# One fused attention, expert and feed-forward kernel: weight tiles converted earlier, token tiles scaled earlier, sums stored in quarters

## The chip, the cores and the metric

The kernel runs on one core of a Trainium2 chip. The metric is the device time of one execution in microseconds. A core has a matrix engine (TensorE, PE in the rows), VectorE (DVE), ScalarE (ACT), GpSimd (POOL) and SyncE (SP), each with an instruction queue of its own that is worked off in order. SyncE computes nothing here: it issues most of the transfers between DRAM and the on-chip memory, and GpSimd issues the rest.

## The reference

Three layers follow one another on 2304 tokens (4 batches of 576), 512 wide. All arrays are 32-bit floats.

```
proj = x @ w_phi; proj -= max|proj|; phi = concat(exp(proj), exp(-proj))      # for q and for k
x    = (phi(q) @ (phi(k).T @ v)) / (phi(q) @ sum(phi(k)) + 1e-6)              # attention, 32 heads
e    = argmax(normalised x . normalised expert_emb)                           # one of 8 experts a token
x    = gate * (relu(x @ w1[e]) @ w2[e])                                       # w1 512x1024, w2 1024x512
h    = x @ w_in;  g = h * sigmoid(h);  out = g @ w_out                        # w_in 512x2048, w_out 2048x512
```

`w_in` and `w_out` arrive as 64-bit floats (the host hands their bytes over as 64-bit whole numbers), so the kernel turns them into 32-bit floats itself.

## The kernel before

A product of 32-bit floats is made of three matmuls in the fast format: each operand is split into a rounded high part (a copy on ScalarE) and the rest (a subtraction on VectorE), and high x high, low x high and high x low are added up (lines 781 to 783). So every block of weights costs a ScalarE copy and a VectorE subtraction before TensorE may use it.

**Slots.** After the attention the tokens are sorted by expert into 22 slots of 128. Slot s fetches its tokens (`gather`), turns them (`xturn`, tile `pxt`), multiplies by w1 (`mm1`, four steps k), applies relu, turns again (`hturn`) and multiplies by w2 (`mm2`, four steps i). The program interleaves neighbours: in round s stand `mm1(s, 0..3)`, then `mm2(s-1, 0..3)`, and between their steps the splits of the next weights (`split(s+1, 1, k)`, `split(s, 2, i)`). The expert weights come in through SyncE (`load1`, `load2`, tiles `raw`); a load is skipped where the expert stays the same.

**Conversion.** `narrow` turns one 128-column tile of `w_in` (or 128 rows of `w_out`) from 64 to 32 bits in four steps, one on ScalarE (line 194) and three on VectorE (lines 199 to 206); `cload` fetches a raw tile, `cwork` does the next step, `cstore` writes the result to DRAM. Tiles 0 to 9 of `w_in` are converted during the attention, 10 to 13 in rounds 5 to 16 (three rounds each), 14 and 15 in units 1 and 2 of the last layer (`sload`). `add_weights` lets GpSimd add stored tiles up in DRAM (three transfers per pair of tiles, each waiting for the one before).

**Units.** The last layer takes the tokens in four blocks of 576 (k) and `w_in` in eight pairs of tiles (q): 32 units u = 8k + q. In a unit seven products stand in for eight (Strassen's scheme in Winograd's form). The order in `unit` is 1, 5, 4 of the unit before, 6, 3 of the unit before, 2, 7. Products 1, 6, 7 and 4 run on in one accumulator `puA`, and after each `keep` copies it out on ScalarE (line 1062) before TensorE may add to it again; products 5, 3 and 2 are added by `join` on VectorE (line 1067). The results stand in two tiles of half a unit, `ha` and `hb`, four buffers in all, and `hstore` writes each to DRAM when both of its halves are in (`hd`, line 1073, SyncE).

`wfetch`, `whigh`, `wlow` bring in and split a pair of `w_in` tiles for a unit. `xfetch`, `xscale`, `xprep` bring in a token tile of a block (tile `yt`), scale it by its gate on VectorE (only the first six tiles of all, line 979) and turn it on TensorE (`pt`, line 988), after which ScalarE copies it out of the one bank that `pt` and `pxt` share (line 994). Block 0 goes through this in rounds 18 to 20, where all of it stands behind a step i of `mm2`. What else stands between the products of a unit is set by hand: `at(u, n, task)` puts a task behind product n of unit u. The 16 tiles of `w_out` are converted in units 8 to 26 that way (`oload` behind product 7 of the unit before, the four steps of `cwork` behind products 1, 5, 3 and 2).

Before unit 17 a branch (`tc.If`, line 1562) decides whether three spare slots are needed (`rest`); with these inputs it is not taken. After the units, 18 token tiles go through the gate and the product with `w_out` (`gate`, `down`, `finish`).

Of the kernel before, what the change touches and what calls it, by code (L numbers as in the profile page):

```python
# [19 lines left out]
P = 128  # L20
# [46 lines left out]
def moe_kernel(ctx, tc, qk, v, w_phi, emb, tau, w1, w2, win, wout, out):  # L67
# [172 lines left out]
    def phase_all(ctx):  # L240
# [686 lines left out]
        def cwork(i):  # L927
            if len(J[i]) == 2:
                J[i].append(narrow(J[i][0], J[i][1], nc.scalar, i))
            next(J[i][2], None)  # L930

        def cstore(i):
            keep_weights(i, J.pop(i)[1])

# [120 lines left out]
        def htile(u, name):  # L1055
            if (u, name) not in HT:
                HT[u, name] = pools["ur"].tile([P, 2, TN], F32, tag="h", name="h" + name, bufs=4)
            return HT[u, name]

        def keep(u, n):  # L1060
            b, name, half = {1: ("A", "a", 0), 6: ("A", "a", 1), 7: ("A", "b", 1), 4: ("A", "b", 0)}[n]
            nc.scalar.copy(out=htile(u, name)[:, half], in_=BK[u, b])

        def join(u, n):
            b, name, half = {5: ("C", "b", 1), 3: ("C", "a", 1), 2: ("B", "a", 0)}[n]
            o = htile(u, name)[:, half]
            nc.vector.tensor_tensor(out=o, in0=BK[u, b], in1=o, op=ALU.add)

        def hstore(u):
            k, q = divmod(u, NJP)  # L1070
            for odd, name in ((1, "b"), (0, "a")):
                dma = nc.gpsimd if u == NUNIT - 1 else nc.sync
                dma.dma_start(out=hd[k][2 * q + odd], in_=HT.pop((u, name)).rearrange("p a t -> p (a t)"))

        def unit(u, todo, skip=()):
            v = u - 1
            for n, w in ((1, u), (5, u), (4, v), (6, u), (3, v), (2, u), (7, u)):
                live = 0 <= w < NUNIT
                if live and (n, w) not in skip:
                    prod(w, n)  # L1080
                if live and n in (1, 6, 7, 4):
                    keep(w, n)
                if n == 5 and v >= 0:
                    join(v, 5)
                if live and n in (3, 2):
                    join(w, n)
                if live and n == 3:
                    hstore(v)
                for f, *a in todo.pop((u, n), ()):
                    f(*a)  # L1090
# [5 lines left out]

        def sload(i):
            if "s" not in J:
                J["s"] = pools["ur"].tile([P, 7 * 512], F32, tag="wb", name="wbs", bufs=4)
            o = (i % 2) * 1024  # L1100
            J[i] = [J["s"][:, o:o + 1024].bitcast(I32).rearrange("p (f t) -> p f t", t=2),
                    J["s"][:, 2048 + o // 2:2560 + o // 2].bitcast(I32)]
            fetch_raw(i, J[i][0])
# [305 lines left out]
        for s in range(1, NSF + 1):  # L1409
# [7 lines left out]
            if s < NSF:  # L1417
# [3 lines left out]
                if q < NJP - 1:  # L1421
                    add_weights(q, n)
                i, n = divmod(s - 5, 3)
                i += CA
                if s == 4:
                    cload(CA)
                for k in range(4):
                    mm1(s, k)
                    if (s, k) == RANK:
                        ranks(B - 1, rbank)  # L1430
                    route(1, s, k)
                    if s + 1 < NSF and k < 3:
                        split(s + 1, 1, k)
                    if 5 <= s < 17 and k == 1 and n == 0:
                        cwork(i)
                    if s == NSF - 1:
                        for f, *a in TAIL[k]:
                            f(*a)
# [13 lines left out]
            for i in range(4):  # L1452
# [11 lines left out]
                if i == 1 and 5 <= s < 17:  # L1464
                    cwork(CA + (s - 5) // 3)
                if i in (1, 2) and 18 <= s < 21:
                    n = 2 * (s - 18) + i - 1
                    if n < 5:
                        xscale(0, n)
# [9 lines left out]
            if 5 <= s < 17 and (s - 5) % 3 == 2:  # L1479
                i = CA + (s - 5) // 3  # L1480
                cstore(i)
                if s < 16:
                    cload(i + 1)
# [15 lines left out]
        htile(0, "a")  # L1499
        wfetch(2)  # L1500
        wfetch(3)
        sload(14)
        sload(15)
# [3 lines left out]
        def plan():  # L1507
            for q in range(2, NJP):
                at(q - 2, 6, whigh, q)
                at(q - 1, 5, wlow, q)  # L1510
                if q + 2 < NJP - 1:
                    at(q - 1, 4, wfetch, q + 2)
            at(5, 1, wfetch, NJP - 1)
# [45 lines left out]
        for u in range(NUNIT):  # L1559
            if u == 17:  # L1560
# [57 lines left out]
```

## Time and profile before

| | |
|---|---|
| median of 3 runs | 1013.27 us (1011.70 to 1014.08) |
| profiled execution, its own time | 1012.02 us |
| its span, first to last instruction | 1010.3 us |
| TensorE busy | 927.1 us, 92% |
| VectorE, ScalarE, GpSimd busy | 613.0, 588.0 and 250.3 us |
| mean granted TensorE clock | 0.97 of full speed |

The span has four stretches: the attention (to about 240 us), the slots (to about 555), the units (to about 800) and the products with `w_out` (to the end). Times in rows count from the start of the span. A wait row says which engine and line waited for which, then the sum, the number of times and the longest, in us.

### The profile page before, as it was taken

To read this page: it belongs to the slowest core of one execution; us is meant where nothing else is said; L and a number is where in the kernel's file an instruction comes from. 1 tells how busy PE (TensorE), PEld (TensorE's weight loads), DVE (VectorE), ACT (ScalarE), POOL (GpSimd) and SP (SyncE) were. 2 spreads that over 40 slices of the span, in tenths; PEclk is the share of its full clock that TensorE was granted. 3 is DMA by queue.
4 is the path that set the end of the run, shared out by engine and by line. 5 is a ranking of instruction groups with operands and counts; after the bars stand their busy time and mean duration, and the time that the engine had idled before them with its cause. 6 is when DMAs were issued, how large, how long until landed. Compare 5 with 4: busy or idle time off the path is not lost. (4 is left out here: it accounts for less than half of the span.)

```text
span 1010.3 us, 15487 instructions
## 1 busy us (share of the span) xinstructions
PE 927.1 (92%) x5567; PEld 801.6 (79%) x5567; DVE 613.0 (61%) x948; ACT 588.0 (58%) x963; POOL 250.3 (25%) x219
## 2 busy tenths in 40 slices
PE   8999999999999999999669596997988899999996
PEld 6999999977777777777557586886987888888885
DVE  6888897877999897797557353552554321112120
ACT  6778878648786897697556343442444443343441
POOL 6887878322015121221000030101000000010100
PEclk9999999999999999999789797998998999999999
DMA  6444534477579559739751784654666654333320
GB/s 177 137 135 143 151 106 132 142 283 219 157 232 259 144 177 336 246 72 290 260 177 42 234 230 143 212 197 152 228 227 208 218 156 138 104 105 115 104 73 21
DMA packets 117697, 173.90 MB, mean 172 GB/s; under 512 B 29736, under 2 KB 71848, under 8 KB 117616
## 3 DMA queue, kind: packets, MB, share of 16 engines
q1 hardware_dynamic: 105584, 151.00, 46.0%
q0 software_dynamic: 11952, 21.83, 9.5%
q8 instruction: 45, 0.74, 0.3%
q14 instruction: 36, 0.29, 0.1%
q10 hardware_dynamic: 80, 0.03, 0.0%
HBM read 172.05 MB, written 54.26 MB: 224 GB/s over the span
## 5 line engine op out<-in xcount | busy, mean ns | idle before, releaser
L831 DVE TENSOR_TENSOR wl<-raw,wh 128x1024 fp32r<-128x1024 f32 (+1 forms) x166 | 188.6, 1174 | 58.8 <-ACT wh L830 53.4
L830 ACT CAST wh<-raw 128x1024 fp32r<-128x1024 f32 (+1 forms) x166 | 160.5, 1032 | 31.4 <-DMA raw<-w 16.2
L1156 DVE TENSOR_TENSOR hlt<-gt,hlt 128x1024 fp32r<-128x1024 f32 x34 | 41.7, 1226 | 139.3 <-ACT hlt L1155 139.3
L782 PE MATMUL po<-wob,hlt 128*128 128x512 f32 x272 | 108.5, 399 | 0.0
L781 PE MATMUL po<-wob,hlt 128*128 128x512 f32 x272 | 107.2, 394 | 0.0
L783 PE MATMUL po<-wob,hlt 128*128 128x512 f32 x272 | 106.6, 392 | 0.0
L417 POOL TENSOR_TENSOR kl<-ke,kh 128x640 fp32r<-128x640 f32 x52 | 84.0, 1637 | 30.8 <-issue 23.2
L467 PE MATMUL pnx<-kv,qp 128*128 128x73 f32 x640 | 76.7, 275 | 0.0
L816 POOL DMA_INDIRECT xg<-xd,gidx x22 | 32.1, 1458 | 175.6 <-PE pxt L851 126.8
L1176 ACT COPY os<-po 128x512 f32<-128x512 f32 x17 | 10.0, 586 | 112.0 <-PE po L783 112.0
L467 PEld LDWEIGHTS pnx<-kv,qp 128*128 128x128 f32 x640 | 74.1, 192 | 0.1
L781 PE MATMUL ph<-wh,xh 128*128 128x512 f32 x166 | 67.1, 404 | 0.0
L783 PE MATMUL ph<-wh,xl 128*128 128x512 f32 x166 | 65.4, 394 | 0.6 <-DVE xl L838 0.4
L971 POOL DMA_INDIRECT yt<-yd,yidx x13 | 15.3, 1181 | 199.7 <-PE pt L988 156.9
L782 PE MATMUL ph<-wl,xh 128*128 128x512 f32 x166 | 64.8, 390 | 0.0
L378 DVE TENSOR_REDUCE m<-pqk 128x10 f32<-128x1280 f32 x32 | 47.5, 1485 | 24.3 <-PE pqk L372 22.9
L1177 POOL DMA_INDIRECT out<-os,oidx x18 | 17.5, 974 | 179.1 <-ACT os L1176 174.2
L781 PEld LDWEIGHTS po<-wob,hlt 128*128 128x128 f32 x272 | 51.1, 188 | 13.3
L783 PEld LDWEIGHTS po<-wob,hlt 128*128 128x128 f32 x272 | 51.1, 188 | 12.3
L782 PEld LDWEIGHTS po<-wob,hlt 128*128 128x128 f32 x272 | 51.1, 188 | 11.6
L372 PE MATMUL pqk<-wbd,zh 128*128 128x256 f32 (+1 forms) x320 | 59.5, 285 | 0.8 <-DVE d L379 0.6
L402 ACT ACTIVATE ke<-d 128x640 f32<-128x640 f32 x52 | 38.3, 737 | 36.8 <-DVE d L379 36.8
(407 smaller groups left out, 2503.6 us busy)
## 6 DMA issues: line engine op xcount, KB each, us to landing
raw<-w SPq DMA_DIRECT2D x44, 1536.0 KB
raw<-w SPq DMA_DIRECT2D x44, 512.0 KB
gt<-hd SPq DMA_DIRECT2D x11, 1024.0 KB
z<-qk SPq DMA_DIRECT2D x32, 288.0 KB
hd<-hb SPq DMA_DIRECT2D x31, 288.0 KB
hd<-ha SPq DMA_DIRECT2D x31, 288.0 KB
wo<-wout SPq DMA_DIRECT2D x16, 512.0 KB
yd<-ys SPq DMA_DIRECT2D x23, 256.0 KB
```

The costliest lines, as they stand in the source:

```text
L372: nc.tensor.matmul(out=pqk[0:r, c * 256:(c + 1) * 256], lhsT=z[:, c * P:c * P + r], rhs=wbd[:, j].rearrange("p h f -> p (h f)"), start=(i ...
L378: nc.vector.tensor_reduce(out=m, in_=pv, axis=AX.X, op=ALU.max, apply_absolute_value=True)
L402: nc.scalar.activation(out=ke, in_=kd, func=AF.Exp, scale=1.0 - 2.0 * s)
L417: nc.gpsimd.tensor_tensor(out=kl[:, :, s, :], in0=st.pop(("ke", g, s)), in1=kh[:, :, s, :].bitcast(F32), op=ALU.subtract)
L467: nc.tensor.matmul(out=pn[:, c, 0:73], lhsT=qp[:, s, c * P:(c + 1) * P], rhs=kv[:, s, 0:73], start=(s == 0), stop=(s == 1))
L781: nc.tensor.matmul(out=o, lhsT=ah, rhs=bh, start=first, stop=False, skip_group_check=more)
L782: nc.tensor.matmul(out=o, lhsT=ah, rhs=bl, start=False, stop=False, skip_group_check=more)
L783: nc.tensor.matmul(out=o, lhsT=al, rhs=bh, start=False, stop=last, skip_group_check=more)
L816: nc.gpsimd.indirect_dma_start(out=xg, out_offset=None, in_=xd[0:n, :], in_offset=bass.IndirectOffsetOnAxis(ap=gidx[:, p:p + 1], axis=0))
L830: nc.scalar.copy(out=hi[:, 0:n], in_=sl[:, 0:n])
L831: nc.vector.tensor_tensor(out=lo[:, 0:n], in0=sl[:, 0:n], in1=hi[:, 0:n].bitcast(F32), op=ALU.subtract)
L1156: nc.vector.tensor_tensor(out=lo, in0=g, in1=hi.bitcast(F32), op=ALU.subtract)
```

## The change

It has six edits.

- **Conversion in the slots.** `convert` does one step each half round from round 2 on, five half rounds per tile (four steps, then the store and the next load). So all six tiles 10 to 15 are done by round 16, where four were before. `sload` and the conversion in units 1 and 2 go; the last pair's `add_weights` stand in round 21.
- **Scaling apart from turning.** `xscale` of block 0 stands behind `mm1` steps 2 and 3, `xprep` behind `mm2` steps 2 and 3 (both stood behind steps 1 and 2 of `mm2`).
- **Quarters.** `ha` and `hb` become single sums `ht` of 128x288, eleven buffers, each stored as soon as its last copy or addition is done: four transfers of 144 KB a unit in place of two of 288 KB.
- **`w_out`.** The step of line 194 is done on VectorE (line 196), the four steps stand in pairs behind products 3 and 2, and the load three or four products earlier, behind product 4. The list of units leaves out two units of 19 where it left out three, so it now has 17 entries: the last one, unit 26, converts tile 0 of `w_out` once more and writes the same values.
- **Token tiles** 0 and 1 of blocks 1 to 3 are fetched behind product 1 in place of 7 of unit 8(k-1)+1, and the last pair of `w_in` behind product 4 of unit 4 in place of product 1 of unit 5.
- **The branch** stands before unit 7.

```diff
         def cwork(i):
             if len(J[i]) == 2:
-                J[i].append(narrow(J[i][0], J[i][1], nc.scalar, i))
+                J[i].append(narrow(J[i][0], J[i][1], nc.scalar if i < NJ else nc.vector, i))
             next(J[i][2], None)
...
+        def convert(n):
+            i, n = divmod(n - 4, 5)
+            if not 0 <= i < NJ - CA:
+                return
+            if n < 4:
+                cwork(CA + i)
+            else:
+                cstore(CA + i)
+                if CA + i + 1 < NJ:
+                    cload(CA + i + 1)
...
-        def htile(u, name):
-            if (u, name) not in HT:
-                HT[u, name] = pools["ur"].tile([P, 2, TN], F32, tag="h", name="h" + name, bufs=4)
-            return HT[u, name]
+        def htile(u, at):
+            if (u, at) not in HT:
+                HT[u, at] = pools["ur"].tile([P, TN], F32, tag="h", name="ht", bufs=11)
+            return HT[u, at]
...
+            nc.scalar.copy(out=htile(u, at), in_=BK[u, "A"])
+            if n == 4:
+                hstore(u, at)
...
             nc.vector.tensor_tensor(out=o, in0=BK[u, b], in1=o, op=ALU.add)
-        def hstore(u):
+            hstore(u, at)
...
+            dma = nc.gpsimd if u == NUNIT - 1 else nc.sync
+            dma.dma_start(out=hd[k][2 * q + at[0]][:, at[1] * TN:(at[1] + 1) * TN], in_=HT.pop((u, at)))
...
-                if q < NJP - 1:
-                    add_weights(q, n)
...
+                add_weights(q, n)
+                if s == NSF - 1:
+                    for q, n in ((NJP - 1, 0), (NJP - 1, 1), (NJP - 1, 2)):
+                        add_weights(q, n)
...
-                    if 5 <= s < 17 and k == 1 and n == 0:
-                        cwork(i)
+                    if k == 1:
+                        convert(2 * s)
+                    if k > 1 and 18 <= s < 21 and 2 * (s - 18) + k - 2 < 5:
+                        xscale(0, 2 * (s - 18) + k - 2)
...
-                if i in (1, 2) and 18 <= s < 21:
-                    n = 2 * (s - 18) + i - 1
+                if i == 1 and s < NSF:
+                    convert(2 * s + 1)
+                if i > 1 and 18 <= s < 21:
+                    n = 2 * (s - 18) + i - 2
                     if n < 5:
-                        xscale(0, n)
                         xprep(0, n)
...
-            for i in (14, 15):
-                for n in (1, 5, 3, 2):
-                    at(i - 13, n, cwork, i)
-                at(i - 13, 7, cstore, i)
-            for n, (u, m) in enumerate(((2, 7), (3, 6), (4, 1))):
-                at(u, m, add_weights, NJP - 1, n)
...
-                at(u + 1, 7, xfetch, k, 0)
-                at(u + 1, 7, xfetch, k, 1)
+                at(u + 1, 1, xfetch, k, 0)
+                at(u + 1, 1, xfetch, k, 1)
...
-            units = [u for u in range(8, 27) if u not in (15, 17, 23)]
+            units = [u for u in range(8, 27) if u not in (15, 23)]
             for j, u in enumerate(units):
-                at(u - 1, 7, oload, j)
+                at(u - 1, 4, oload, j)
             for j, u in enumerate(units):
-                for n in (1, 5, 3, 2):
+                for n in (3, 3, 2, 2):
                     at(u, n, cwork, NJ + j)
...
-            if u == 17:
+            if u == NJP - 1:
```

Three places show how instructions move. The first is VectorE in round 18, from the token tile of slot 19 (`xl`) to the end of `hturn(18)` (`hl`); `wl1` and `wl2` are split weights, `yt` the scaled token tiles. Before:

```order
L838 TENSOR_TENSOR xl_6019<-pxt_6013,xh_6018 128x512
L831 TENSOR_TENSOR wl1_6024<-raw1_1_2791,wh1_6023 128x1024
L831 TENSOR_TENSOR wl2_6045<-raw2_0_158,wh2_6044 128x1024
L831 TENSOR_TENSOR wl2_6075<-raw2_0_158,wh2_6074 128x1024
L979 TENSOR_SCALAR yt_5884<-yt_5884,gate_s_142 128x512
L831 TENSOR_TENSOR wl2_6096<-raw2_0_158,wh2_6095 128x1024
L979 TENSOR_SCALAR yt_5886<-yt_5886,gate_s_142 128x512
L831 TENSOR_TENSOR wl2_6113<-raw2_0_158,wh2_6112 128x512
```

The same place in the changed kernel:

```order
L990 TENSOR_SCALAR yt_5898<-yt_5898,gate_s_142 128x512
L990 TENSOR_SCALAR yt_5900<-yt_5900,gate_s_142 128x512
L838 TENSOR_TENSOR xl_6035<-pxt_6029,xh_6034 128x512
L831 TENSOR_TENSOR wl1_6040<-raw1_0_2790,wh1_6039 128x1024
L831 TENSOR_TENSOR wl2_6061<-raw2_0_158,wh2_6060 128x1024
L831 TENSOR_TENSOR wl2_6091<-raw2_0_158,wh2_6090 128x1024
L831 TENSOR_TENSOR wl2_6101<-raw2_0_158,wh2_6100 128x1024
L831 TENSOR_TENSOR wl2_6119<-raw2_0_158,wh2_6118 128x512
```

Both scalings have moved ahead of `xl` and of the three or four subtractions of weights behind which they stood.

The second is SyncE's queue in units 0 and 1, from the load of the fourth pair of `w_in` (`sscr3`) on. Before:

```order
L949 DMA ws_6627<-sscr3_70 128x1792
L169 DMA wbs_6629<-win 128x4x256 x2
L949 DMA ws_6685<-sscr4_71 128x1792
L1073 DMA hd0_83<-hb_6656 128x576
L1073 DMA hd0_83<-ha_6624 128x576
L181 DMA sscr7_74<-wbs_6629 128x512
L182 DMA sscr7_74<-wbs_6629 128x256
L969 DMA yt_6725<-yd_66 128x512
L969 DMA yt_6727<-yd_66 128x512
```

The same place in the changed kernel:

```order
L960 DMA ws_6644<-sscr3_70 128x1792
L1086 DMA hd0_83<-ht_6641 128x288
L980 DMA yt_6683<-yd_66 128x512
L980 DMA yt_6685<-yd_66 128x512
L1086 DMA hd0_83<-ht_6672 128x288
L1086 DMA hd0_83<-ht_6703 128x288
L960 DMA ws_6706<-sscr4_71 128x1792
```

The raw tiles 14 and 15 are gone, and the two token tiles stand ahead of the fifth pair of `w_in`, behind one quarter store.

The third is ScalarE around the start of unit 8, where `xcT` and `xcB` are high parts of token sums and `ha`, `hb`, `ht` the copies of `keep`. Before:

```order
L1062 COPY hb_7150<-puA_7087 128x288
L1024 CAST xcT3_7152<-xf_6741 128x576
L1062 COPY ha_7164<-puA_7157 128x288
L194 ACTIVATE wo_7155<-wo_7155 128x512
L1062 COPY hb_7150<-puA_7087 128x288
```

The same place in the changed kernel:

```order
L1073 COPY ht_7627<-puA_7558 128x288
L1035 CAST xcT3_7629<-xf_6754 128x576
L1073 COPY ht_7639<-puA_7632 128x288
L1073 COPY ht_7656<-puA_7558 128x288
L1035 CAST xcT4_7659<-xf2_7102 128x576
```

No step of the conversion stands between the copies of `keep` any more.

## Rows read from the trace of the kernel before

**Rows 1.** The page's head: span and instructions.
```profile
span 1010.3 us, 15487 instructions
```

**Rows 2.** TensorE's waits from 470 to 560 us, rounds 18 to 21.
```profile
PE pt L988 <- DVE yt L979: 18.7, 5, 6.9
```

**Rows 3.** TensorE's waits from 560 to 630 us, units 1 to 5.
```profile
PE puA L781 <- ACT hb L1062: 13.2, 2, 9.8
PE pt L988 <- DVE yt L979: 6.4, 2, 6.2
```

**Rows 4.** TensorE's waits from 630 to 820 us, the later units.
```profile
PE puA L781 <- ACT ha L1062: 13.8, 12, 2.9
PE pt L988 <- DMA yt<-yd,yidx: 5.6, 1, 5.6
PE puC L781 <- DVE hb L1067: 2.7, 1, 2.7
```

**Rows 5.** Stretches: start:end, length, busy us per engine (instructions), granted clock, DMA share, GB/s.
```profile
250.00:470.00 220.00, 215.46 (x1036) 166.15 (x1035) 197.98 (x278) 176.87 (x259) 51.07 (x37) 1.00 0.71 207
550.00:800.00 250.00, 204.85 (x1400) 197.26 (x1399) 120.33 (x206) 103.21 (x208) 18.94 (x16) 0.92 0.60 196
710.00:740.00 30.00, 29.88 (x226) 29.52 (x226) 17.75 (x35) 14.89 (x35) 1.89 (x2) 1.00 0.64 225
```

**Rows 6.** Timeline of TensorE: start us, us, the turning of each slot's tokens.
```profile
302.88 0.60 PE L851 MATMUL pxt<-ident,xg 128*128 128x128 f32 x4
...
461.69 0.60 PE L851 MATMUL pxt<-ident,xg 128*128 128x128 f32 x4
474.12 0.60 PE L851 MATMUL pxt<-ident,xg 128*128 128x128 f32 x4
500.97 0.60 PE L851 MATMUL pxt<-ident,xg 128*128 128x128 f32 x4
...
522.41 0.60 PE L851 MATMUL pxt<-ident,xg 128*128 128x128 f32 x4
```

**Rows 7.** Timeline of all engines in round 18; in brackets idle before and releaser.
```profile
479.28 2.94 ACT L830 CAST wh<-raw 128x1024 fp32r<-128x1024 f32 x3 [3.82 <-DMA raw<-w]
...
483.77 0.48 DVE L979 TENSOR_SCALAR yt<-yt,gate_s 128x512 f32<-128x512 f32 x1
...
484.40 1.08 PE L988 MATMUL pt<-ident,yt 128*128 128x128 f32 x4 [6.93 <-DVE yt L979]
```

**Rows 8.** Timeline of all engines in unit 5.
```profile
613.49 1.68 ACT L956 CAST wbr<-ws 128x1792 fp32r<-128x1792 f32 x1 [11.28 <-DMA hd<-hb]
...
615.52 0.61 PE L781 MATMUL puA<-xcT,wbr 128*128 128x288 f32 x1 [9.78 <-ACT hb L1062]
```

**Rows 9.** The stored sums' tensor `hd`: who waited for it; issue to landing.
```profile
ACT ha L1062: 25.5, 10
...
DMA to landing us min/median/max: 5.4/5.5/5.6
```

**Rows 10.** The tile `wo`: duration in ns (min/median/max), and who waited for it.
```profile
L194 ACT ACTIVATE wo<-wo x16: 672/692/710, 631.7 to 758.9; 128x512 f32<-128x512 f32 x16
L202 DVE TENSOR_SCALAR wo<-wo x16: 428/429/432, 631.7 to 758.9; 128x512 int32<-128x512 int32 x16
L206 DVE SCALAR_TENSOR_TENSOR wo<-wo x16: 679/682/687, 636.0 to 764.1; 128x512 int32<-128x512 int32 x16
...
ACT wo L194: 34.4, 15
```

**Rows 11.** Timeline: token tiles of blocks 1 and 3 fetched, scaled, turned.
```profile
575.78 0.49 DVE L979 TENSOR_SCALAR yt<-yt,gate_s 128x512 f32<-128x512 f32 x1 [6.03 <-DMA yt<-yd]
...
695.00 0.94 POOL L971 DMA_INDIRECT yt<-yd,yidx  x1 [41.57 <-PE puA L783]
...
700.62 1.08 PE L988 MATMUL pt<-ident,yt 128*128 128x128 f32 x4 [5.62 <-DMA yt<-yd,yidx]
```

**Rows 12.** The tile `yt`: us from a fetch's issue to its landing.
```profile
DMA to landing us min/median/max: 3.3/4.6/9.0
```

More of the change, by code (lines that the diff above doesn't have):

```diff
@@ L1053, in prod, with hstore @@
                 three(o, wh[:, ws], wl[:, ws], xc[:, 0, c], xc[:, 1, c], first and c == 0, c == 1, not first)
-        def htile(u, name):
-            if (u, name) not in HT:
-                HT[u, name] = pools["ur"].tile([P, 2, TN], F32, tag="h", name="h" + name, bufs=4)
-            return HT[u, name]
+        def htile(u, at):
+            if (u, at) not in HT:
+                HT[u, at] = pools["ur"].tile([P, TN], F32, tag="h", name="ht", bufs=11)
+            return HT[u, at]
         def keep(u, n):
-            b, name, half = {1: ("A", "a", 0), 6: ("A", "a", 1), 7: ("A", "b", 1), 4: ("A", "b", 0)}[n]
-            nc.scalar.copy(out=htile(u, name)[:, half], in_=BK[u, b])
+            at = {1: (0, 0), 6: (0, 1), 7: (1, 1), 4: (1, 0)}[n]
+            nc.scalar.copy(out=htile(u, at), in_=BK[u, "A"])
+            if n == 4:
+                hstore(u, at)
         def join(u, n):
-            b, name, half = {5: ("C", "b", 1), 3: ("C", "a", 1), 2: ("B", "a", 0)}[n]
-            o = htile(u, name)[:, half]
+            b, at = {5: ("C", (1, 1)), 3: ("C", (0, 1)), 2: ("B", (0, 0))}[n]
+            o = htile(u, at)
             nc.vector.tensor_tensor(out=o, in0=BK[u, b], in1=o, op=ALU.add)
-        def hstore(u):
+            hstore(u, at)
+        def hstore(u, at):
             k, q = divmod(u, NJP)
-            for odd, name in ((1, "b"), (0, "a")):
-                dma = nc.gpsimd if u == NUNIT - 1 else nc.sync
-                dma.dma_start(out=hd[k][2 * q + odd], in_=HT.pop((u, name)).rearrange("p a t -> p (a t)"))
+            dma = nc.gpsimd if u == NUNIT - 1 else nc.sync
+            dma.dma_start(out=hd[k][2 * q + at[0]][:, at[1] * TN:(at[1] + 1) * TN], in_=HT.pop((u, at)))
         def unit(u, todo, skip=()):
@@ L1086, in unit @@
                     join(w, n)
-                if live and n == 3:
-                    hstore(v)
                 for f, *a in todo.pop((u, n), ()):
@@ L1095, in oload @@
             fetch_raw(NJ + j, J[NJ + j][0])
[L1097 to L1103, printed above, removed]
         WO = {}
@@ L1420, in phase_all @@
                 q, n = divmod(s - 1, 3)
-                if q < NJP - 1:
-                    add_weights(q, n)
[L1423 to L1426, printed above, removed]
+                add_weights(q, n)
+                if s == NSF - 1:
+                    for q, n in ((NJP - 1, 0), (NJP - 1, 1), (NJP - 1, 2)):
+                        add_weights(q, n)
                 for k in range(4):
@@ L1463, in phase_all @@
                     load1(s + 2, (1,))
-                if i == 1 and 5 <= s < 17:
-                    cwork(CA + (s - 5) // 3)
-                if i in (1, 2) and 18 <= s < 21:
-                    n = 2 * (s - 18) + i - 1
+                if i == 1 and s < NSF:
+                    convert(2 * s + 1)
+                if i > 1 and 18 <= s < 21:
+                    n = 2 * (s - 18) + i - 2
                     if n < 5:
-                        xscale(0, n)
                         xprep(0, n)
@@ L1478, in phase_all @@
                 yout(s - 1)
[L1479 to L1483, printed above, removed]
+            if s == 1:
+                cload(CA)
             if s == NSF - 1:
@@ L1497, in at @@
             todo.setdefault((u, n), []).append(task)
-        htile(0, "a")
+        htile(0, (0, 0))
         wfetch(2)
         wfetch(3)
-        sload(14)
-        sload(15)
         at(0, 5, xsum, 0, "T4")
@@ L1510, in plan @@
                 at(q - 1, 5, wlow, q)
-                if q + 2 < NJP - 1:
+                if q + 2 < NJP:
                     at(q - 1, 4, wfetch, q + 2)
-            at(5, 1, wfetch, NJP - 1)
-            for i in (14, 15):
-                for n in (1, 5, 3, 2):
-                    at(i - 13, n, cwork, i)
-                at(i - 13, 7, cstore, i)
-            for n, (u, m) in enumerate(((2, 7), (3, 6), (4, 1))):
-                at(u, m, add_weights, NJP - 1, n)
             for k in range(1, NT // (2 * TN)):
                 u = NJP * (k - 1)
-                at(u + 1, 7, xfetch, k, 0)
-                at(u + 1, 7, xfetch, k, 1)
+                at(u + 1, 1, xfetch, k, 0)
+                at(u + 1, 1, xfetch, k, 1)
                 for n, (v, m) in enumerate(((2, 1), (3, 1), (3, 6), (4, 6), (5, 4))):
```

## The prediction

> **What bounds the kernel now.** I began with the page's head [rows 1]: the span is 1010.3 us, and TensorE is busy in 92% of it, so about 83 us are left in which it idles. A faster kernel has to take those, or the time that TensorE runs at the low clock. The next view, by stretches, says where they are [rows 5]. In the slots (250 to 470 us) TensorE is busy 215.5 of 220 us at full clock: nothing to win there. The units (550 to 800) are different: 204.85 busy of 250, so 45.15 idle, and a granted clock of 0.92. From 710 to 740, the same work runs with 0.1 us of idle in 30 at clock 1.00, with 226 matmuls in 29.88 us, 132 ns each. So the units can run without waits.
>
> The waits of TensorE name the causes. In rounds 18 to 21 it waits 18.7 us in five pieces for the scaling of a token tile on VectorE [rows 2]. In units 1 to 5 it waits 13.2 us for a copy of `keep` on ScalarE and 6.4 for a scaling [rows 3]. In the later units it waits 13.8 us in twelve pieces for `keep` and 5.6 once for a token tile's fetch [rows 4].
>
> Then I followed the large ones back. In round 18 TensorE stands 6.93 us before `pt`. The scaling takes only 0.48 us, but stands in VectorE's queue behind splits of weights, which wait for ScalarE's casts, which waited 3.82 us for the transfer of `raw` [rows 7]. The token tile itself is not what is late. In unit 5 ScalarE's copy of `keep` stands behind `whigh` of the last pair, which had idled ScalarE for 11.28 us [rows 8]. The row names a store of `hd` as the releaser, but the program has `whigh` wait for the load of `ws`, which waits for GpSimd's last addition to that pair, and tiles 14 and 15 of that pair are the two converted in units 1 and 2. I take that for the cause. In the other units two things hold `keep` up: ScalarE waits for a buffer whose store has not landed (25.5 us in ten waits; the landing takes 5.5 us) [rows 9], and for the load of a `w_out` tile (34.4 us in 15 waits) [rows 10].
>
> **The change, part by part.**
>
> Scaling ahead of the splits. The turnings of successive slots stand at 461.69, 474.12, 500.97 and 522.41 [rows 6]. So a round without token tiles takes 12.43 us, and rounds 18 and 19 took 26.85 and 21.44. With two turnings of 0.60 an undisturbed round takes 13.6. The excess is 13.2 + 7.8 = 21.0, waits and low clock together. Round 20 holds the fifth wait; I take the mean of the four shorter ones, (18.7 - 6.93) / 4 = 2.9. Together 23.9. What is late next: the one bank that `pt` uses. The second turning of round 18 has to wait until ScalarE has copied the first, and that copy stands behind the late casts: 479.28 + 2.94 for three [rows 7], one more cast of 1.0 and a copy of 0.6 end at 483.8. TensorE gets there at about 481.2 (477.5, where it stopped before, two `mm2` steps at an eighth of a round each, a turning). So 2.6 us stay. The term is 23.9 - 2.6 = **21 us gained**; bounds 24 (no such wait) and 15 (the clock falls once more).
>
> Units. I take as gone: 9.8 of the 13.2 [rows 3, 8], since the last pair is complete in DRAM long before its load; 6.2 of the 6.4, since the fetch goes out most of a unit earlier, where VectorE had waited 6.03 us for it [rows 11]; 12 of the 13.8 [rows 4], since both causes go (eleven quarters let a store lag more than two units, and ScalarE no longer waits for `w_out`); and the 5.6, whose fetch left GpSimd only at 695.00, after 41.57 us of waiting [rows 11], behind the branch. The branch now stands ten units earlier and the fetch six products earlier. Sum 33.6 of 45.15. The clock costs 0.08 x 204.85 = 16.4 us there [rows 5]; the removed waits' share of it is 0.74 x 16.4 = 12.2. Together 45.8. What stays: the first load of unit 0 (3.4 of the 13.2), 2.7 at the end [rows 4], and small ones. Which wait stands behind a removed one the trace can't show; its price lies between nothing (710 to 740 has none) and half of the term. I take 4, near the first since that stretch is the nearest. The term is **42 us gained**. As a check, 1400 matmuls at 132 ns are 185 us, and 185 + 11.6 of waits that stay + 4 of low clock + 4 is 205, 45 less than 250.
>
> Two more tiles in the slots. Twelve rounds from 302.88 to 461.69 took 158.8 us and converted four tiles [rows 6]; twelve rounds of 12.43 are 149.2. So a tile cost at most 2.4 us, and two more cost 4.8. Their VectorE steps are 0.43 + 2 x 0.68 = 1.8 us [rows 10], in a stretch where VectorE has 22 us free in 220 [rows 5], so nothing is possible too. Bounds 0 and 8; I take **3 us lost**.
>
> What costs nothing. The multiplication moved to VectorE: between 0.43 and 0.69 us [rows 10], 17 times, under VectorE's 130 idle us in the units [rows 5]; it costs this much a unit where VectorE is full. Its load has nine products in place of one, so the wait for it can move to VectorE, where only stores and additions queue behind it. The 17th tile: 2.3 us of VectorE and 0.75 MB, once. The 62 extra stores: SyncE's queue, and nothing but loads waits behind them. If a load waits there, `whigh` does, and so does `keep`.
>
> A rule speaks against the quarters. A store takes 5.5 us to land, and ten waits hang on that [rows 9]. The Trainium skill ("DMA: Bandwidth & Descriptors", "Rules for kernel authors") says to coalesce many small transfers into one large one, and its "Anatomy of one DMA" gives 2.0 us fixed plus the bytes over 436 GB/s. By that, four stores of 147 KB take an estimated 9.4 us a unit and two of 295 KB took 5.4; one after another, they would hold a unit of some 7.8 us to 9.4, and the time would be about 1045. The trace does not agree that they go one after another: the 5.5 us of landing did not keep units from running at 132 ns a matmul in the stretch 710 to 740 [rows 5, 9].
>
> The sum, against the profiled execution's own 1012.0 us (span 1010.3, 1.7 around it): 1012.0 - 21 - 42 + 3 = 952. The median of the runs stands 1.3 higher, so 953.
>
> **The rivals.**
>
> *The scaling waits for its own tile.* Tiles 2 and 3 of block 0 are fetched a step later and scaled three steps earlier: half a round, 6.8 us, where there was a whole one. A fetch lands in 3.3 to 9.0 us [rows 12]. At 9.0 VectorE waits about 2 us, and TensorE, which needs nothing of it for half a round, does not. For: DMA is full there, a late `raw` shows it [rows 7]. Against: the median is 4.6. At twice the longest, 18 us, TensorE loses 18 - 2 x 6.8 = 4.4 in each of rounds 19 and 20, some 6 with the clock: 965.
>
> *A second wait stands behind the first in the units.* ScalarE still has splits, copies and casts between the copies of `keep`, and VectorE's steps now stand in pairs. For: twelve small waits, not one large. Against: the stretch 710 to 740. With half of the 45.8 left, 952 + 23 - 4 = 971.
>
> *Slower: the stores bind.* SyncE's transfers use eight semaphores in turn, so each waits until the eighth before it has landed. A unit has four stores, a load and a store of `w_out` and half a token tile, 6.5 transfers. With a landing of L a unit can't be shorter than 6.5 L / 8: at 5.5 us [rows 9] 4.5, below the 5.6 of 42 matmuls at 132 ns; from 6.9 us on it binds. The whole gain is lost where a unit takes 8.4 us (250 / 32 + 18 / 32), that is from a landing of 10.3 us on; at 11 us a unit takes 8.9, and the time is 1029. For: more, smaller transfers in less time. Against: the DMA engines are busy only 0.60 there [rows 5].
>
> *It doesn't reach what it aims at.* If `whigh` of the last pair did wait for a store of `hd`, as its row says, that wait may stay; all of them staying, and the slots gaining nothing, would be no change.
>
> **How the numbers follow.** The forecast has 0.67, the late tile 0.13, the second wait 0.14, the binding stores 0.04, no change 0.02. The likeliest case alone runs from 942 to 965 (slots 15 to 24, units 36 to 46, conversion 0 to 8). The range is 940 to 972: it takes in the centres of the first two rivals, and leaves out the outer part of the second, the other two, and the tails, some 0.19. Faster by over 0.2% (about what a measurement of this kernel can tell from none) has 0.94, within it 0.02, slower 0.04.
>
> **What would show it.** Right: the turnings of slots 19 to 21 stand under 15 us apart; TensorE waits for scalings under 3 us; no wait of ScalarE for `hd` or `w_out`; the units take 205 to 210 us. Wrong: a scaling with a wait for its fetch ahead of it, with `pt` or `mm1` of the next round idle behind; `hd` landing in 7 us or more; TensorE's waits for `keep` still above 8 us in sum; slots of rounds 2 to 16 more than 8 us longer in all.

## The result and the profile after

The changed kernel takes **958.51 us** (median of 4 runs, 957.49 to 960.73) where the kernel before took 1013.6 beside it: a ratio of 0.9463, 95% interval 0.9442 to 0.9484. The profiled execution took 958.07 us. The time was forecast at 953.0 and lies in the range, 5.5 us above the forecast.

The page's head answers to [rows 1]. Instructions of TensorE are as many as before; its idle time fell from 83 us to 43.

```profile
span 956.4 us, 15631 instructions
...
PE 913.1 (95%) x5567; PEld 794.5 (83%) x5567; DVE 620.0 (65%) x968; ACT 581.7 (61%) x947; POOL 253.8 (27%) x221
```

The starts of the slots' turnings, as in [rows 6], say what became of the slots. Rounds 18 and 19 took 14.88 and 13.33 us where they took 26.85 and 21.44. The twelve rounds from 302.36 took 158.47 us with six tiles' conversion in rounds 2 to 16, where they took 158.81 with four.

```profile
302.36 0.60 PE L851 MATMUL pxt<-ident,xg 128*128 128x128 f32 x4
...
460.83 0.60 PE L851 MATMUL pxt<-ident,xg 128*128 128x128 f32 x4
473.27 0.60 PE L851 MATMUL pxt<-ident,xg 128*128 128x128 f32 x4
488.15 0.60 PE L851 MATMUL pxt<-ident,xg 128*128 128x128 f32 x4
...
501.48 0.60 PE L851 MATMUL pxt<-ident,xg 128*128 128x128 f32 x4
```

TensorE's waits from 530 to 780 us, all units and the first steps of the last stretch, answer to [rows 3, 4]. No token tile is waited for any more. The 13.2 and 13.8 us for copies of sums have become 9.3. The second, third and fourth row are new or dearer.

```profile
PE puA L781 <- ACT ht L1073: 9.3, 8, 3.8
PE puC L781 <- DVE ht L1080: 6.3, 2, 5.2
PE po L781 <- ACT hlt L1158: 3.3, 1, 3.3
PE puA L781 <- PEq L1552: 2.5, 1, 2.5
```

So I followed those back. The timeline around 734 us shows the load of `g` (the first sums, for the gate) leaving SyncE at 723.33, behind four stores of quarters; ScalarE can start on it 6.3 us later. ScalarE waits 2.45 us for it, then does its 1.91 us activation, and only behind that and a cast the two copies of sums that TensorE needs. At 755 it is the same with the second load: it can leave only at 746.44, when TensorE has done the last product of the units, and ScalarE waits 6.93 us for it.

```profile
716.72 6.56 SPq L1086 DMA_DIRECT2D hd<-ht  x4
723.33 0.43 SPq L1135 DMA_DIRECT2D g<-hd  x1
...
729.67 1.91 ACT L1146 ACTIVATE g<-g 128x2048 f32<-128x2048 f32 x1 [2.45 <-DMA g<-hd]
731.62 1.04 ACT L1158 CAST hl<-g 128x1024 fp32r<-128x1024 f32 x1
732.57 0.69 ACT L1073 COPY ht<-puA 128x288 f32<-128x288 f32 x2
...
733.84 0.45 DVE L1080 TENSOR_TENSOR ht<-puC,ht 128x288 f32<-128x288 f32 x1
...
734.34 0.61 PE L781 MATMUL puC<-xcB,wbr 128*128 128x288 f32 x1 [5.16 <-DVE ht L1080]
...
746.44 3.10 SPq L1135 DMA_DIRECT2D gt<-hd  x3
...
752.95 1.06 ACT L1154 ACTIVATE gt<-gt 128x1024 f32<-128x1024 f32 x1 [6.93 <-DMA gt<-hd]
...
755.14 0.50 PE L781 MATMUL po<-wob,hlt 128*128 128x512 f32 x1 [3.32 <-ACT hlt L1158]
```

SyncE's own waits name what the second load stood for; in the kernel before, that load (`gt`) had left at 798.80, ahead of the last product at 806.19, and ScalarE had not waited for it:

```profile
SPq L1135 <- PE puC L783: 9.4, 1, 9.4
```
```profile
798.80 29.26 SPq L1132 DMA_DIRECT2D gt<-hd  x7
...
806.19 0.29 PE L783 MATMUL puC<-xcB,wbr 128*128 128x288 f32 x1
```

Behind both waits of TensorE the granted clock is 0.55 and 0.66 in the five us that follow, and in the first case 1.00 again behind them (columns as in [rows 5]).

```profile
735.00:740.00 5.00, 5.00 (x21) 4.81 (x21) 1.84 (x4) 0.40 (x1) 0.60 (x1) 0.55 0.35 119
740.00:745.00 5.00, 5.00 (x25) 4.17 (x24) 0.00 (x0) 0.00 (x0) 0.56 (x1) 1.00 0.09 31
...
755.00:760.00 5.00, 4.34 (x11) 3.13 (x12) 2.45 (x2) 2.09 (x3) 0.00 (x0) 0.66 0.67 209
```

### The profile page after: what moved, and what is told of

It reads as the page before. It is cut to its first block, busy times and chain, and to the rows that moved or that the text cites. A ratio compares the mean times of both kernels' runs of the same rounds, so it can differ in the third digit from the quotient of the medians.

```text
span 956.4 us, 15631 instructions
## 1 busy us (share of the span) xinstructions
PE 913.1 (95%) x5567; PEld 794.5 (83%) x5567; DVE 620.0 (65%) x968; ACT 581.7 (61%) x947; POOL 253.8 (27%) x221
## 5 line engine op out<-in xcount | busy, mean ns | idle before, releaser
L1073 ACT COPY ht<-puA 128x288 f32<-128x288 f32 x128 | 50.1, 400 | 94.0 <-PE puA L783 84.5
L816 POOL DMA_INDIRECT xg<-xd,gidx x22 | 34.8, 1584 | 173.5 <-PE pxt L851 131.6
```

What stands on the lines that cost most here:

```text
L1073: nc.scalar.copy(out=htile(u, at), in_=BK[u, "A"])
```

## The experiments

My theory was the prediction's: the parts add up, the scaling some 21 us and the units the rest, with two things that hold ScalarE in the units (stores of `hd` and loads of `w_out`). The rivals are in the expectations below. Times are medians. The kernel before took 1011.8 to 1012.6 us beside these runs and 1013.6 beside the kernel after, so a difference of two us between two rows tells nothing.

| kernel | us | ratio to before, 95% interval |
|---|---|---|
| after | 958.51 | 0.9463 (0.9442 to 0.9484) |
| before + scaling | 988.64 | 0.9758 (0.9733 to 0.9783) |
| after, scaling as before | 980.66 | 0.9686 (0.9661 to 0.9712) |
| before + conversion in the slots | 1004.98 | 0.9917 (0.9892 to 0.9942) |
| after, four halves | 980.29 | 0.9674 (0.9648 to 0.9699) |
| after, five halves | 958.64 | 0.9476 (0.9444 to 0.9509) |
| after, eight quarters | 959.64 | 0.9464 (0.9422 to 0.9505) |
| after, `w_out` as before | 990.43 | 0.9775 (0.9741 to 0.9809) |
| after, four halves and `w_out` as before | 977.32 | 0.9648 (0.9620 to 0.9677) |
| after, only the multiplication on ScalarE | 958.77 | 0.9469 (0.9442 to 0.9497) |
| after, branch and fetches as before | 965.89 | 0.9543 (0.9511 to 0.9576) |
| after, earlier loads for the gate | 950.58 | 0.9400 (0.9375 to 0.9425) |
| the same, branch ahead of unit 15 | 953.23 | 0.9418 (0.9394 to 0.9441) |

**The scaling, added alone and taken away alone.** In the kernel before:

```diff
+                    if k > 1 and 18 <= s < 21 and 2 * (s - 18) + k - 2 < 5:
+                        xscale(0, 2 * (s - 18) + k - 2)
...
-                if i in (1, 2) and 18 <= s < 21:
-                    n = 2 * (s - 18) + i - 1
+                if i > 1 and 18 <= s < 21:
+                    n = 2 * (s - 18) + i - 2
                     if n < 5:
-                        xscale(0, n)
                         xprep(0, n)
```

> The kernel before, with one part of the change alone: the token tiles of block 0 are scaled half a slot ahead of their turning. Theory (the parts add up, and this one takes VectorE's queue of splits out of TensorE's way): the five waits for a scaling in rounds 18 to 21 go, the starts of slots 19 and 20 stand under 15 us after the ones before them, and the time falls by 21 us (18 to 24), to about 992. Rival (the raw weights arrive late there and TensorE would stop for their splits as soon as it no longer stops for the scaling): the rounds stay at 20 us or more, and the time falls by less than 8 us.

Measured: 988.64, 23.5 us less. All five waits for a scaling are gone. One wait stands in their place, for ScalarE's copy out of the bank that the turnings share, 2.0 us:

```profile
PE pt L988 <- ACT xf L994: 2.0, 1, 2.0
```

Slots 19, 20 and 21 start at 471.66, 487.25 and 500.58 us: 15.59 us, a little over the 15 that was expected, and 13.33. The same lines taken out of the kernel after:

> The kernel after, with the scaling alone put back just before each turning, as before. Theory (parts add up): the waits for the scaled tile come back, 18 to 24 us, so 977 to 983 us. Rival (with tiles 14 and 15 and their loads gone from the start of the units, that place is less crowded and the scaling would have come early enough without being moved): within 5 us of the kernel after, under 964.

Measured: 980.66, 22.1 us more. The term is the same from both sides within the noise, so it does not depend on the other parts, and both rivals fall. Both runs move the turnings by one step as well as the scalings, so they price the two together.

**Conversion in the slots alone.** In the kernel before, `sload` and the steps of tiles 14 and 15 in units 1 and 2 go, and the additions of the last pair with them:

```diff
-            for i in (14, 15):
-                for n in (1, 5, 3, 2):
-                    at(i - 13, n, cwork, i)
-                at(i - 13, 7, cstore, i)
-            for n, (u, m) in enumerate(((2, 7), (3, 6), (4, 1))):
-                at(u, m, add_weights, NJP - 1, n)
...
+                    if k == 1:
+                        convert(2 * s)
```

> The kernel before, with one part alone: all w_in tiles converted by slot 16, so nothing of w_in is left for units 1 to 5; halves of sums, w_out, branch and fetches as before. Theory (whigh of the last pair waited for that pair's additions, not for a store of hd as its row says): ScalarE's wait of 11.28 us in unit 5 and TensorE's 9.78 behind it go, though the sums are still stored in halves from four buffers; the slots cost at most 1 us more, and the time falls by 9 to 15 us, to about 1001. Rival (the row is right and the store of hd holds ScalarE): the wait stays, and the time stays within 3 us of before, 1011 to 1017.

Measured: 1004.98, 7.2 us less, a little short of what was expected. The wait of ScalarE in [rows 8] is gone, though sums are still stored in halves from four buffers. Its waits from 560 to 640 us, where the kernel before had 11.3 us on line 956, now have 0.5 on that line (967 here) and 4.5 as the longest for a store:

```profile
ACT wo L194 <- DMA wo<-wout: 10.1, 4, 3.1
ACT ha L1073 <- DMA hd<-hb: 7.1, 2, 4.5
...
ACT wbr L967 <- DMA ws<-sscr: 0.5, 1, 0.5
```

So the releaser that the row named, a store of `hd`, was not the cause; the late conversion and additions of the last pair were. In the slots six tiles cost no more than four: the twelve rounds of [rows 6] take 158.04 us here. Part of the 9.8 us came back, most of it at the end: the gate's second load now waits for the last product of the units, and TensorE waits 4.0 us behind it.

```profile
SPq L1143 <- PE puC L783: 8.8, 1, 8.8
```
```profile
PE po L781 <- ACT hlt L1166: 4.0, 1, 4.0
```

The kernel before and the one with the scaling alone do not have this wait. Every other kernel here with the conversion in the slots and the gate's loads at their old place has it, 3.2 to 4.1 us, with long units and with short ones. So it is a price of this edit. The edit takes `sload`'s tile out of the buffers of the split pairs; that the second load's buffer thereby came to lie where the last product still reads is what I take from the program, and no run shows it.

**Quarters, and what in them helps.** First the kernel after with the halves back:

```diff
-            HT[u, at] = pools["ur"].tile([P, TN], F32, tag="h", name="ht", bufs=11)
+            HT[u, name] = pools["ur"].tile([P, 2, TN], F32, tag="h", name="h" + name, bufs=4)
...
+                if live and n == 3:
+                    hstore(v)
```

> The kernel after, with the sums back in halves: four buffers of two sums each, both halves of a unit stored after product 3 of the next, as before. Theory (the eleven quarter buffers take ScalarE's wait for landed stores away): ScalarE waits for hd again some 20 us in all, TensorE waits for copies of sums 5 to 10 us more, and the time rises by 6 to 14 us, to 965 to 973. Rival 1 (once ScalarE no longer waits for w_out the stores have time, and the quarters were not needed): 956 to 961. Rival 2 (twice as many stores of half the size cost the transfers more than they free): under 955.

Measured: 980.29, 21.8 us more, beyond the 6 to 14 expected. Then the same memory in eight quarters, and five halves (only the numbers of buffers change, 11 to 8 and 4 to 5):

> The kernel after, with eight quarter buffers in place of eleven, which is the memory of the four halves of before: only the early store of each quarter is left of that part. The kernel with four halves took 980 us, 22 more than after. Theory A (a sum's buffer comes free sooner because each quarter is stored as soon as it is joined, instead of after product 3 of the next unit): most of the 22 us stays gained, 959 to 968 us, ScalarE waits for hd under 20 us. Theory B (the memory is what counts: eleven quarters let a store lag by half again as much as four halves): most of the 22 us is lost, 971 to 982 us, and ScalarE waits for hd 30 us or more.

> The kernel after with the sums in halves, with five buffers (the memory of ten quarters) in place of four. Theory A (the early store of quarters is what frees ScalarE): a fifth half helps somewhat, 966 to 978 us. Theory B (memory counts): within 4 us of the kernel after, 955 to 962 us. The rule that few large stores cost less than many small ones would give at most 955.

Measured: 959.64 and 958.64. Neither theory holds as stated: the early store alone gives the whole gain, and so does one more buffer alone. One explanation fits both: a copy waits where its buffer is wanted sooner after the store's issue than the store lands. A product takes some 0.79 us (42 matmuls of 132 ns by 7). With four halves the buffer is wanted three products after the store, 2.4 us, and the 20 copies that ScalarE held back for a store began 4.1 to 7.3 us after that store's issue, 4.7 in the middle. With five halves it is nine products or more, 7.1 us, and with eight quarters at least six, 4.8 us. ScalarE's waits for stores from 590 to 740 us, 42.3 us with four halves (row below), shrink to 0.6 with five, and with eight quarters there is none. Once above, more gives nothing.

```profile
ACT ha L1073 <- DMA hd<-ha: 0.6, 2, 0.3
```

The landing that the view of `hd` gives is no measure of this: it covers only transfers of the last unit, which GpSimd issues, and none of SyncE's. When the quarters landed in the units is therefore not shown.

The quarters have a price at the gate's first load. In the kernels with quarters and that load at its old place ScalarE waits for it 0.7 to 2.5 us, and TensorE's wait behind it is 3.5 to 5.2 us; in all kernels with halves ScalarE does not wait, and TensorE's wait is 2.6 or 2.7, as before. With five halves, whose units are as short as with quarters, the load leaves 7.9 us before ScalarE comes to it; in the kernel after it leaves 3.9 us before, since in SyncE's queue it stands behind quarters that wait for their sums:

```profile
720.44 0.43 SPq L1135 DMA_DIRECT2D g<-hd  x1
```
```profile
728.30 1.92 ACT L1146 ACTIVATE g<-g 128x2048 f32<-128x2048 f32 x1
```

**`w_out`, alone and together with the halves.** The kernel after with the old conversion of `w_out`:

```diff
-                J[i].append(narrow(J[i][0], J[i][1], nc.scalar if i < NJ else nc.vector, i))
+                J[i].append(narrow(J[i][0], J[i][1], nc.scalar, i))
...
-                at(u - 1, 4, oload, j)
+                at(u - 1, 7, oload, j)
...
-                for n in (3, 3, 2, 2):
+                for n in (1, 5, 3, 2):
```

> The kernel after, with the conversion of w_out as before: multiplication on ScalarE behind product 1, its load only one product earlier, the steps behind products 1, 5, 3, 2 (17 tiles as after). Theory (ScalarE's waits for w_out loads hold up copies of sums even when no copy waits for a store): ScalarE waits 25 to 40 us for w_out again, TensorE waits for copies some 5 to 9 us more, and the time rises by 6 to 12 us, to 964 to 971. Rival (with free buffers for its copies ScalarE has slack for these waits, each under 3.5 us): 957 to 961.

Measured: 990.43, 31.9 us more, far beyond the 6 to 12 expected. Undone together with the quarters:

> The kernel after, with both parts undone that were undone singly before: sums in four halves and the conversion of w_out on ScalarE with its late load. Undone singly, the halves cost 22 us (980.3) and w_out 32 us (990.4). Theory (both hold ScalarE, and a wait for the one passes while it waits for the other, so the costs do not add up; from the kernel before, less 23.5 for the scaling, 7.2 for the slots and up to 7 for branch and fetches): 975 to 985 us, so that the quarters without the change to w_out would be a loss. Rival (the costs add up): 1005 to 1018 us.

Measured: 977.32. The theory holds, and more sharply than it was put. All four corners are now measured:

| | `w_out` as before | `w_out` as after |
|---|---|---|
| four halves | 977.32 | 980.29 |
| eleven quarters | 990.43 | 958.51 |

With halves, the change to `w_out` is worth nothing (3 us dearer, and the intervals overlap). With the old `w_out`, the quarters cost 13 us. Together they save 18.8. ScalarE's waits from 590 to 740 us show why, first with both as before, then with halves and the new `w_out`, then with quarters and the old `w_out`:

```profile
ACT wo L194 <- DMA wo<-wout: 34.6, 16, 2.8
...
ACT ha L1073 <- DMA hd<-hb: 10.7, 4, 4.1
```
```profile
ACT ha L1073 <- DMA hd<-hb: 42.3, 16, 6.6
```
```profile
ACT wo L194 <- DMA wo<-wout: 51.1, 16, 5.0
```

Take the wait for `w_out` away, and ScalarE comes earlier to the copy whose buffer has not landed and waits there instead: 42.3 us in place of 45. Take the waits for stores away, and the wait for `w_out` grows by half. In the kernel after, little is left of either in the same window:

```profile
ACT ht L1073 <- DMA hd<-ht: 4.3, 10, 0.4
```

Why it grows is in SyncE's queue. In the kernel with quarters and the old `w_out` the load stands behind four stores, each of which waits for its sum. It leaves at 660.36, after ScalarE has already been idle for 0.55 us (4.98 before 664.79):

```profile
653.45 6.86 SPq L1086 DMA_DIRECT2D hd<-ht  x4
660.36 0.42 SPq L169 DMA_DIRECT2D wo<-wout  x1
...
664.79 0.67 ACT L194 ACTIVATE wo<-wo 128x512 f32<-128x512 f32 x1 [4.98 <-DMA wo<-wout]
```

With halves, the load of the corresponding unit leaves at 654.86, 1.1 us before ScalarE comes to it:

```profile
654.86 0.38 SPq L169 DMA_DIRECT2D wo<-wout  x1
...
658.57 0.69 ACT L194 ACTIVATE wo<-wo 128x512 f32<-128x512 f32 x1 [2.62 <-DMA wo<-wout]
```

The last of this group takes back only the engine: the first line of the diff above, with the early load and the late steps kept.

> The kernel after, with the multiplication of w_out on ScalarE, but loaded as early and stepped through as late as in the kernel after. Theory (the 32 us came from the load, issued one product ahead of its use behind four stores of quarters in SyncE's queue, not from the engine): ScalarE waits under 8 us for w_out, and the time is 957 to 962 us. Rival (an extra 0.68 us for 17 units and a wait on ScalarE is what hurts): 965 us or more.

Measured: 958.77, no change that can be measured. ScalarE waits for `w_out` 2.8 us in two waits. So of this edit the earlier load and the later steps count, which no run takes apart, and the move to VectorE gives nothing.

**Branch and fetches as before.** (With the branch ahead of unit 17, that unit converts no `w_out` tile.)

```diff
-                at(u + 1, 1, xfetch, k, 0)
-                at(u + 1, 1, xfetch, k, 1)
+                at(u + 1, 7, xfetch, k, 0)
+                at(u + 1, 7, xfetch, k, 1)
...
-            if u == NJP - 1:
+            if u == 17:
```

> The kernel after, with the branch ahead of unit 17 again and the fetches of each block's first two token tiles behind product 7 again (and no w_out tile in unit 17: 16 tiles in place of 17). Theory (the fetch of block 3 stands in GpSimd's queue behind the branch, that of block 1 comes too late for its turning): TensorE waits 5 to 6 us for each of the two, the 2.5 us at the branch ahead of unit 7 go, and the time rises by 7 to 12 us, to 965 to 971. Rival (these fetches were late only because the transfers of w_in tiles and the stores of sums held the queues; those are gone or earlier): 955 to 960.

Measured: 965.89, 7.4 us more, and both waits are back, somewhat shorter than expected: 4.59 for block 1's scaling and 3.76 for block 3's fetch, which GpSimd issues only 4.94 us ahead of the turning. Branch and fetches were undone together, so the run does not say which of the two makes this fetch late. TensorE's wait at the branch is gone from its list.

```profile
648.40 0.95 POOL L982 DMA_INDIRECT yt<-yd,yidx  x1 [35.85 <-PE puB L783]
```
```profile
552.48 1.11 PE L999 MATMUL pt<-ident,yt 128*128 128x128 f32 x4 [4.59 <-DVE yt L990]
...
653.34 0.68 PE L999 MATMUL pt<-ident,yt 128*128 128x128 f32 x4 [3.76 <-DMA yt<-yd,yidx]
```

**Earlier loads for the gate.** The two late waits of the kernel after point to a better version, with both loads moved at once:

```diff
-            first = p == h == 0
+            first = p == 0
...
-            at(30, 1, gload, 0, 0)
+            at(28, 1, gload, 0, 0)
...
+            at(31, 3, gload, 0, 1)
...
-        gload(*loads[1])
```

> The kernel after, with the first two loads for the down projection issued earlier: that of the first 256 tokens' first half behind product 1 of unit 28 instead of 30, that of their second half behind product 3 of unit 31 into the buffer that the first leaves, instead of after the units' buffers are given back. Theory (the 5.16 us wait at 734 and the 3.32 at 755 each end a chain that begins with such a load, and the low clock behind each is their doing): both fall under 1.5 us, the matmuls behind them run at full clock, and the time falls by 7 to 12 us, to 946 to 952 us. Rival (the Silu and casts on ScalarE, 1.91 and 1.04 us, hold up the copies of sums wherever the load stands): 955 to 959 us.

Measured: 950.58, 7.9 us less than the kernel after; the intervals do not touch. In TensorE's waits of the same stretch the row for `hlt` is gone, and the longest for VectorE is 2.6 us where it was 5.2 (the theory said under 1.5). From 730 to 760 us the granted clock is 0.94 where it was 0.83; the theory had full clock.

```profile
PE puA L781 <- ACT ht L1073: 7.7, 9, 2.1
PE puC L781 <- DVE ht L1080: 4.2, 3, 2.6
PE puA L781 <- PEq L1553: 2.7, 1, 2.7
```
```profile
730.00:760.00 30.00, 27.38 (x138) 23.86 (x138) 7.51 (x10) 11.11 (x15) 2.46 (x5) 0.94 0.62 184
```

Then the branch ahead of unit 15 as well (`if u == 15:`):

> The kernel before this one in the list (earlier loads for the down projection), with the branch also moved from ahead of unit 7 to ahead of unit 15, which converts no w_out tile and has no block's fetches right behind it. Theory (the 2.5 us at the branch come from the engines meeting there while TensorE has only just restarted, and ahead of unit 17 it had cost 0.33): 1 to 3 us less than the kernel with the earlier loads alone. Rival (the branch costs the same wherever it stands): within 1 us of it.

Measured: 953.23, its interval overlapping the one above. TensorE's wait at the branch is 2.6 us there, as it was 2.7 ahead of unit 7. Moving it there gives nothing, as the rival said. But a branch does not cost the same wherever it stands: ahead of unit 17 it was 0.33 in the kernel before, and too little to be listed in the run with branch and fetches as before.

## Why the prediction was right, and where it was off

Measured against the profiled execution, the sum was 60 us (1012.0 to 952), and 53.9 came (to 958.07). It is told by the steps of the prediction.

- **Scaling, 21 gained: right.** 23.5 added alone, 22.1 taken away alone. The wait that was to stay behind it, 2.6 us for ScalarE's copy at the second turning of round 18, is there: 2.0 alone, 1.3 in the kernel after.
- **Two more tiles in the slots, 3 lost: nothing.** The rounds are 0.3 us shorter (158.47 against 158.81). Of the bounds the lower one was right: VectorE had room for the steps. By the start of slot 21 the kernel had gained 20.9 us where the prediction's terms make 15.4 (21.0 for rounds 18 and 19, less 2.6 and 3; its fifth wait for a scaling, 2.9, comes behind that start). What the prediction did not see is that this edit would hold up the gate's second load.
- **`whigh` of the last pair, 9.8: the cause was right,** against the releaser in the row; the conversion alone removes the wait. But alone it gives 7.2 us, as 4.0 of it are waited at the second load.
- **The copies of sums, 12 of 13.8: the mechanism was right.** "Both causes go" was the condition, and the runs show how much hangs on *both*: with the quarters alone this term would have been a loss of 13 us, and with the change to `w_out` alone nothing. What I had called a second wait behind the first is what each half of the change would have met. It wasn't met, because the two were made together. The landing of 5.5 us [rows 9] was misread, as it is that of two transfers of GpSimd behind the last unit. The ten copies held back in the kernel before began 2.2 to 6.4 us after the issue of the store they waited for, 4.5 in the middle, so the size was near by luck.
- **Fetches of token tiles, 6.2 and 5.6: right.** Both waits are gone, and undoing them together with the branch brings 4.59 and 3.76 back and 7.4 us in all.
- **What stays, "I take 4", and nothing behind the units: these are the steps that failed.** From the start of slot 21 to the end the prediction's terms make 44.9 (42 and the fifth wait of 2.9), and 33.0 came, 12 short. That the slots gave 5.5 more than their terms made up for nearly half of it, which is luck. The units, from product 6 of unit 0 to the last product, went from 250.2 to 215.0 us, so 35.2 of the 42 came. There TensorE waits 2.5 us more at the gate's first load (5.16 in place of 2.7) and 2.2 more at the branch (2.5 in place of 0.33 ahead of unit 17), and the low clock behind that load costs some 2.4: from 734.34 on, 18 matmuls and two of the larger ones take 5.28 us where at full clock they take 18 x 0.133 + 2 x 0.227 = 2.85. The last stretch, for which the prediction had no term, went from 204.0 to 210.2 us: 3.3 us of wait for the second load, and some 1.6 of low clock (behind 756.40, eight matmuls take 0.43 each in place of 0.23). That is 12.0, less the 4 allowed 8.0, of the 12 that are missing; the rest was not traced. Shorter units alone make neither load late: with five halves the first is not waited for, and the second is late with long units too. The first is held up by the quarters in SyncE's queue, and the second by the conversion in the slots. I priced the stretch from 710 to 740, where nothing waits, and did not ask which loads at the end the edits would push back. The run with both loads earlier gave 7.9 us back.
- **The branch, moved at no cost: off by 2.2 us.** It costs TensorE 2.5 us ahead of unit 7 here. Why it cost 0.33 ahead of unit 17 is open.
- **The multiplication on VectorE at no cost: right, but it gave nothing either.** The gain that I put down to ScalarE no longer waiting for `w_out` comes from the load standing four products earlier and the steps later, taken together.
- **62 extra stores at no cost: right in sum, wrong at one load.** Five halves, with 62 stores fewer, take 958.64 against 958.51. The queue did matter in the way that I named (a load behind a store that waits): it cost 13 us where the load of `w_out` stayed late, and it is what makes the gate's first load late. What the quarters give back elsewhere was not traced. The Trainium skill's rule on coalescing ("DMA: Bandwidth & Descriptors", "Rules for kernel authors") would have made larger stores the faster ones. No run here shows that: four halves were slower and five were equal. The fit of the Trainium skill with which the prediction priced the rule is stated there for transfers that GpSimd issues, and SyncE issues these.

Of the signs of being right, the rounds are under 15 us, there is no wait of TensorE for a scaling, and of ScalarE's waits for stores 4.3 us are left, at most 0.4 at a time. The units take 215 us, not 205 to 210. One sign of being wrong is there: TensorE's waits for copies of sums still come to 9.3 us, above the 8 named. Of the rivals, the late tile is not in the trace; nor do the stores bind, as several units of the kernel after take 5.6 us, no more than their matmuls. The whole of "a second wait" would have given 971.

## What to carry to other kernels

When two causes hold one engine in turn, removing one moves the wait to the other, and a run with one of them undone says little about the other's worth: measure all four corners before dropping a half that "does nothing". For a buffer, compare the time from the store's issue to the next use with the landing; one step above it was the whole gain here. And follow an edit to the end of its stretch: ask which loads now stand behind its stores in a queue, and which buffers of the next stretch come free later. Most of what was missing here was lost at two such loads.

## What the runs showed of the hardware that I had not expected

A store of 288 KB does not land in a fixed time. In the kernel with four halves the 20 copies that waited for one began 4.1 to 7.3 us after its issue, and in the kernel before ten began 2.2 to 6.4 us after. What sets it was not tested.

A branch that is not taken can make TensorE wait. In the kernels with the branch ahead of unit 7 the wait was 2.3 to 3.5 us, ahead of unit 15 it was 2.6, and ahead of unit 17 it was 0.33. Why the place matters is open.
